# Output stores begun by ScalarE one unit late, and GpSimd's power two slots later, in a fused attention and MLP kernel

## The chip, the cores and the metric

The kernel runs on one NeuronCore of a Trainium2 chip. A core has five engines that each take their instructions in order: TensorE (PE, matmuls), VectorE (DVE), ScalarE (ACT), GpSimd (POOL) and SyncE (SP, which here only begins transfers). They wait for one another through semaphores. The metric is the device time of one execution in microseconds, as the median of several; less is better.

## What is computed

For 8 batches of 8 heads, 576 positions and head width 64: causal attention with a bias from a running sum, then a layer norm over the 512 joined columns, a two-layer MLP (512 to 2048 to 512, ReLU) and a residual.

```python
scores = q @ k.T / sqrt(64)
cum = cumsum(maximum(s, 0));  bias = minimum(-(cum_i - cum_j), 0)
attn = softmax(where(causal, -1e9, scores + bias))
x = (attn @ v)                      # heads joined: (8, 576, 512)
mu, var = mean(x), mean((x - mu) ** 2)
xn = (x - mu) / sqrt(var + 1e-6) * g_ln
out = x + maximum(xn @ w_ch1, 0) @ w_ch2
```

The power in the title is the `(var + 1e-6) ** -0.5` of the layer norm, the deviation. The kernel applies it last: it scales the MLP's result by `rstd` as it adds the residual, which is allowed because ReLU and the matmuls keep a positive factor per row.

## The kernel before

The main loop goes over 64 slots n = 8 b + h, one for each head h of batch b. A slot makes the scores of its head (`sa`, `sb`, `sc`, and in even slots `sd` for the last 64 positions of two heads), their exponentials on ScalarE, the causal masks on GpSimd, and the product with v (`pot`) of the head two slots back. Between these it works off a queue of MLP units of the batch before: 16 units `mlp1` (four matmuls each) and, for each of four row tiles, four units `mlp2`. From batch 3 on a slot takes four units; the `mlp1` units fall into h = 4 to 7 and the `mlp2` units into h = 0 to 3 of the next batch. Two pools of PSUM matter here, each with two buffers, and one SBUF pool of three for finished rows:

```python
yop  = tc.tile_pool(name="yop", bufs=3)
ps_m = tc.tile_pool(name="ps_m", bufs=2, space=PSUM)     # ph and py of the MLP
ps_t = tc.tile_pool(name="ps_t", bufs=2, space=PSUM)     # sd and trx
```

The last block of scores, and the transposes of the normalised rows; both take a buffer of `ps_t`:

```python
def scores_d(b, j):
    ...
    d = ps_t.tile([P, 2, TL], F32, name="sd", tag="tr")
    ...                                            # matmuls into d
    nc.scalar.activation(out=ed, in_=d[0:TL], func=ACT.Exp, scale=scale)
    ...

def ln_tr(b, t, eng="dve"):
    ...
    tr = ps_t.tile([P, KD, P], BF16, name="trx", tag="tr")
    for kd in range(KD):
        nc.tensor.transpose(tr[:, kd, :], xn[:, kd * P : (kd + 1) * P], ident)
    ...
    copy_on(eng, dst, tr)
```

The layer norm's pieces. VectorE does the statistics and `xn`; after the last tile `ln_rstd` adds 1e-6 on VectorE and takes the power on GpSimd:

```python
    def ln_rstd(b):
        n = len(x_tiles(b))
        rs = rstd[:, b, 0:n]
        nc.vector.tensor_scalar_add(out=rs, in0=mvs[b][:, 0:n, 1], scalar1=1e-6)
        nc.gpsimd.tensor_tensor(out=rs, in0=rs, in1=mhalf[:, 0:n], op=ALU.pow)

    def ln_xn(b, t):
        ...                                        # ln_aggr, xn on VectorE
        if b > 0 and t == len(tiles) - 1:
            ln_rstd(b)
```

The last quarter of a tile's `mlp2` finishes its rows on VectorE and hands them to `put`, which begins the store on SyncE:

```python
        if quarter == 3:
            yo = yop.tile([P, Dm], F32, name="yo", tag="yo")[:, 0 : c1 - c0]
            nc.vector.scalar_tensor_tensor(
                out=yo, in0=py[0], scalar=rs, in1=x[:, c0:c1], op0=ALU.mult, op1=ALU.add
            )
            dst(yo, c0, c1)
...
    def batch_units(b):
        def of_t(t):
            def put(yo, c0, c1):
                nc.sync.dma_start(out=out[b, t * P : (t + 1) * P, c0:c1], in_=yo)
            return xb[b][:, t, :], rstd[:, b, t : t + 1], put
        return chunk_units(lambda: xTs[b], of_t)

...
    def run_units(n, dve_first=False):
        for i in range(n):
            if queue:
                first_unit[0] = dve_first and i == 0
                queue.pop(0)()
```

The rows of 64 that are left over from each batch are gathered in pairs and done at the end (`mixed_units`); their stores are begun by SyncE and ScalarE already.

The body of a slot from n = 9 on, and the order within it (the loads and DMA transposes of coming heads, all on SyncE, are begun in `pre(n)`):

```python
def pv_next():
    ...
    pv(pb, ph_)
    ...
    if ph_ == 7:
        ln_open(pb)
        ...
        for t in range({1: 3, B - 1: 1}.get(pb, NT)):
            ln_xn(pb, t)

for n in range(BH):
    b, h = n // H, n % H
    pre(n)
    ...
        scores(b, h)
        run_units(1, True)
        if h % 2 == 0:
            scores_d(b, h // 2)
        run_units(1)
        if n > 9:
            pv_next()
        ...
        lt = {2: (0, 1), 3: (2, 3, 4)}.get(h, ()) if b > 1 else ()
        for t in lt:
            ln_tr(b - 1, t, "act" if b == 2 else "dve")
            if t != 1 and t != 4:
                run_units(1)
                nu -= 1
        ...
        run_units(nu)
        if b > 1 and h == 3:
            run_units(len(queue))
            queue += batch_units(b - 1)
```

So the layer norm of batch b - 1 runs on VectorE in h = 1 of batch b, two slots after its last head, and its transposes stand in h = 2 and h = 3.

Of the kernel before, what the change touches and what calls it, by code (L numbers as in the profile page):

```python
# [15 lines left out]
P = 128  # L16
# [3 lines left out]
def kernel(  # L20
# [11 lines left out]
    nc = tc.nc  # L32
    B, H, S, D = q.shape
# [43 lines left out]
    rstd = const.tile([P, B, NT], F32, name="rstd")  # L77
# [18 lines left out]
    def copy_on(eng, out, in_):  # L96
        if eng == "act":
            nc.scalar.copy(out=out, in_=in_)
        elif eng == "dve":
            nc.vector.tensor_copy(out=out, in_=in_)  # L100
        else:
            nc.gpsimd.tensor_copy(out=out, in_=in_)  # L102
# [140 lines left out]
    def tr_pair(g):  # L243
        tr_kind("k", g)
        tr_kind("q", g)
# [29 lines left out]
    def qk_pair(g, k_engs, q_engs):  # L275
        tr_pair(g)
        evac_pair("k", g, k_engs)
        evac_pair("q", g, q_engs)
# [62 lines left out]
    def scores_d(b, j):  # L341
        u0 = (2 * j) % 4
        pe_mask = b * H + 2 * j < NM
        ed = er[0:TL, u0 : u0 + 2, OD : OD + TL]
        d = ps_t.tile([P, 2, TL], F32, name="sd", tag="tr")
        for u in range(2):
            nc.tensor.matmul(
                d[:, u, :],
                lhsT=k_cols(b, 2 * j + u, NF),
                rhs=q_cols(b, 2 * j + u, NF * P, S)[0][2],  # L350
                start=True,
                stop=not pe_mask,
            )
            if pe_mask:
                nc.tensor.matmul(  # L355
                    d[:, u, :], lhsT=ident, rhs=maskT[:, 0:TL], start=False, stop=True
                )
        nc.scalar.activation(out=ed, in_=d[0:TL], func=ACT.Exp, scale=scale)
        if pe_mask:
            return  # L360
        nc.gpsimd.affine_select(
            out=ed,
            in_=ed,
            compare_op=ALU.is_ge,
            fill=0.0,
            base=0,
            pattern=[[0, 2], [1, TL]],
            channel_multiplier=-1,
        )
# [40 lines left out]
    def x_tiles(b):  # L410
        ts_ = [xb[b][:, t, :] for t in range(NF)]
        if b % 2 == 1:
            ts_.append(xm[b // 2])
        return ts_
# [20 lines left out]
    def ln_rstd(b):  # L435
        n = len(x_tiles(b))
        rs = rstd[:, b, 0:n]
        nc.vector.tensor_scalar_add(out=rs, in0=mvs[b][:, 0:n, 1], scalar1=1e-6)  # L438
        nc.gpsimd.tensor_tensor(out=rs, in0=rs, in1=mhalf[:, 0:n], op=ALU.pow)  # L439

    def ln_aggr(b, t):
        nc.vector.bn_aggr(out=mvs[b][:, t, :], in_=st[b][:, t, 0 : 4 if b == 0 else 3, :])
# [30 lines left out]
    def ln_first_rstd():  # L473
        for t in range(NF):
            ln_aggr(0, t)
        ln_rstd(0)

    def ln_tr(b, t, eng="dve"):
        if (b, t) not in xns:
            return  # L480
        xn = xns.pop((b, t))
# [3 lines that stand above are left out]
        if t < NF:  # L485
            dst = xTs[b][:, :, t * P : (t + 1) * P]
        else:
            dst = xTm[:, :, (b // 2) * P : (b // 2 + 1) * P]
        copy_on(eng, dst, tr)
# [40 lines left out]
    def chunk_units(xT_of, of_t, last=False):  # L530
        units = [lambda fb=fb: mlp1(xT_of(), fb) for fb in range(FB)]
        for t in range(NF):
            halves = ((0, 256), (256, 512)) if last and t == NF - 1 else ((0, 512),)
            for c in halves:
                for qr in range(4):
                    units.append(lambda t=t, qr=qr, c=c: mlp2(t, qr, *of_t(t), *c))
        return units

    def batch_units(b):
        def of_t(t):  # L540
            def put(yo, c0, c1):
                nc.sync.dma_start(out=out[b, t * P : (t + 1) * P, c0:c1], in_=yo)
            return xb[b][:, t, :], rstd[:, b, t : t + 1], put
        return chunk_units(lambda: xTs[b], of_t)

# [7 lines left out]

    queue = []
    pend = []

    def run_units(n, dve_first=False):
        for i in range(n):
            if queue:
                first_unit[0] = dve_first and i == 0  # L560
                queue.pop(0)()

# [30 lines left out]
    for i in range(2):  # L595
# [5 lines left out]
        out=maskT,  # L601
        in_=maskT,
# [18 lines left out]
    for t in range(NT):  # L621
# [5 lines left out]
        out=c_in, in0=c_in, scalar1=0.0, scalar2=1.0 / scale, op0=ALU.max, op1=ALU.mult  # L627
    )
    nc.vector.tensor_tensor_scan(
        out=c_sc, data0=c_one, data1=c_in, initial=0.0, op0=ALU.mult, op1=ALU.add  # L630
# [114 lines left out]
# [3 lines that stand above are left out]
        if n < 8:  # L748
            scores(b, h)
            if h in (1, 3, 5, 6):  # L750
                scores_d(b, h // 2)
            if h in (0, 2, 4):
                qk_pair(h // 2 + 1, ("dve", "dve"), ("act", "dve" if h < 4 else "act"))
            pend.append((b, h))
            if n == 7:
                pv_next()
                tr_pair(4)
                pv_next()
                evac_pair("k", 4, ("act", "act"))
                evac_pair("q", 4, ("act", "act"))  # L760
                trc = bias_tr()
                keep_warm(8)
                continue
            if n % 2 == 1 or n == 0:
                keep_warm(2)
            if n > 1:
                pv_next()
            if n == 6:
                pv_next()
            continue  # L770
        if n == 8:

            phs = [
                pool.tile([P, 512], F32, name="ph", tag=tag)
                for pool, tag in ((ps_m, "m"), (ps_m, "m"), (ps_s, "s"), (ps_s, "s"))
            ]

            def columns(t):
                cols = slice(t * P, (t + 1) * P)
                for fb, ph in enumerate(phs):  # L780
                    for kd in range(KD):
                        nc.tensor.matmul(
                            ph[:, cols],
                            lhsT=w1_bf[:, kd, fb * P : (fb + 1) * P],
                            rhs=xTs[0][:, kd, cols],
                            start=(kd == 0),
                            stop=(kd == KD - 1),
                        )

            for t in range(NF):  # L790
                ln_tr(0, t, "act" if t < 3 else "dve")
                if t > 0:
                    columns(t - 1)
            columns(NF - 1)
            for fb, ph in enumerate(phs):
                if fb % 2 == 0:
                    nc.scalar.activation(out=hT[:, fb, :], in_=ph, func=ACT.Relu)
                else:
                    nc.vector.tensor_scalar_max(out=hT[:, fb, :], in0=ph, scalar1=0.0)
            ln_first_rstd()  # L800
            queue += batch_units(0)[4:]
            scores(b, h)
            scores_d(b, h // 2)
            pend.append((b, h))
            run_units(1)
            continue

        end = next(m for m in (8 * i + 3 for i in range(2, B + 1)) if m >= n)
        nu = (2 if n < 16 else -(-len(queue) // (end - n + 1))) - 2
        if n in PAIRS:  # L810
            qk_pair(PAIRS[n], ("dve", "dve"), ("act", "act"))
# [7 lines that stand above are left out]
        if n == 9:  # L819
            bias_rows(trc)  # L820
        pend.append((b, h))
# [6 lines that stand above are left out]
        if n == 2 * H + 2:  # L828
            for t in range(3, NT):
                ln_xn(1, t)  # L830
        run_units(nu)
        if b > 1 and h == 3:
            run_units(len(queue))
            queue += batch_units(b - 1)
    pv_next()
# [3 lines left out]
    for t in range(NT):  # L839
        ln_xn(B - 1, t + 1)  # L840
        run_units(1)
        ln_tr(B - 1, t, "act")
    run_units(len(queue))
    queue += batch_units(B - 1)
    queue += mixed_units()
# [30 lines left out]
```

The softmax here doesn't subtract the row's maximum and nothing guards it: scores larger than these inputs give would overflow.

## Time and profile before

| what | value |
|---|---|
| time, median of 3 | 367.94 us (367.81 to 368.48) |
| span of the profiled run | 366.8 us |
| mean granted TensorE clock | 0.998 |
| TensorE busy (matmuls) | 97% of the span |
| VectorE, ScalarE, GpSimd busy | 55%, 52%, 45% |
| store of finished rows (`out_dram<-yo`) by SyncE | 32 of 256 KB, 0.36 us median to begin one |
| GpSimd's power (`rstd<-rstd,mhalf`) | 8, 1.1 us each |

In the profile's lines PE is TensorE, PEld its weight loads, DVE is VectorE, ACT ScalarE, POOL GpSimd and SPq SyncE's queue. L followed by a number is the line of the kernel. `py<-w_bf,hT` names what is written and what is read. Timeline lines begin with the start and the duration in microseconds; x8 at the end counts instructions merged into one line; a bracket gives the idle time before it and what ended it. In the list of waits the three numbers are microseconds in total, the number of waits and the longest.

### The profile page before, as it was taken

Reading aid. Unit: us, or ns where it says so; the run is one execution under the profiler, and the core shown is the slowest. Engines: PE = TensorE matmul, PEld = TensorE weight load, DVE = VectorE, ACT = ScalarE, POOL = GpSimd, SP = SyncE. Lnnn points to the kernel's source line nnn. Section 1 sums busy time; section 2 is a strip of 40 time slices with the busy share of each in tenths; the row PEclk is TensorE's granted clock in tenths of the full one; section 3 lists DMA queues with packets and bytes.
Section 4 is the critical chain, followed back from the end, with each engine's and each line's share of the span. In section 5 each row is a group of like instructions: output and inputs, shape, how many; then the busy total and the mean of one; then the engine's idle time right before and its main releaser. Section 6 shows DMA issues by size and latency. Waiting matters only on the chain.

```text
span 366.8 us, 8315 instructions
## 1 busy us (share of the span) xinstructions
PE 355.0 (97%) x3017; PEld 197.1 (54%) x3067; DVE 202.9 (55%) x535; ACT 191.3 (52%) x367; POOL 164.9 (45%) x447
## 2 busy tenths in 40 slices
PE   8998999999999999999999999999999999999995
PEld 3677555565555555555455555555555554444444
DVE  7697789684357554944384547743675483112211
ACT  5895988467732673367534753476337522501410
POOL 8854468667633656344675563554852101000000
PEclk9999999999999999999999999999999999999999
DMA  8999999999965999599979986798830011011013
GB/s 144 162 195 178 202 211 193 163 240 176 183 146 141 206 199 181 104 215 163 188 176 213 194 183 140 189 191 182 174 102 2 0 59 57 1 58 59 0 31 86
DMA packets 156653, 52.17 MB, mean 142 GB/s; under 512 B 143641, under 2 KB 151940, under 8 KB 156612
## 3 DMA queue, kind: packets, MB, share of 16 engines
q1 hardware_dynamic: 138868, 43.08, 55.5%
q0 software_dynamic: 17344, 8.03, 18.9%
q8 instruction: 24, 0.39, 0.5%
q10 hardware_dynamic: 400, 0.52, 0.4%
q14 instruction: 17, 0.14, 0.2%
HBM read 37.11 MB, written 9.44 MB: 127 GB/s over the span
## 4 chain that ended last, share of the span: by engine, by line
PE 72%; DVE 7%; DMA 6%; SPq 4%; POOL 4%; issue 3%; ACT 3%; POOLq 0%; ACTq 0%
PE py L515 26%; PE ph L497 25%; PE pot L389 6%; SPq L164 3%; PE sc L312 3%; PE sa L312 3%; PE sb L312 3%; DMA rowtmp<-in_q_dram 2%; PE idle L568 2%; DMA vtmp<-in_v_dram 2%; DVE xn L451 2%; PE trx L484 2%; DVE stats L423 1%; POOL er L331 1%; ACT er L323 1%
## 5 line engine op out<-in xcount | busy, mean ns | idle before, releaser
L515 PE MATMUL py<-w_bf,hT 128*128 128x512 bf16 (+1 forms) x565 | 132.1, 373 | 1.6 <-DVE yo L524 0.4
L497 PE MATMUL ph<-xT,w_bf 128*128 128x512 bf16 x478 | 116.4, 379 | 1.1 <-DVE yo L524 0.2
L507 ACT ACTIVATE hT<-ph 128x512 bf16<-128x512 f32 x102 | 61.0, 598 | 64.4 <-PE ph L497 64.4
L515 PEld LDWEIGHTS <-hT 128*128 128x128 bf16 x592 | 53.5, 98 | 49.1 <-issue 0.9
L497 PEld LDWEIGHTS <-w_bf 128*128 128x128 bf16 x560 | 50.1, 97 | 51.3 <-issue 2.9
L323 ACT ACTIVATE er<-sa 128x512 bf16<-128x512 f32 x64 | 38.2, 597 | 70.9 <-PE sa L312 50.1
L331 POOL TENSOR_SCALAR_AFFINE_SELECT er<-er 128x128 bf16<-128x128 bf16 x216 | 59.7, 300 | 22.5 <-ACT er L323 22.3
L505 DVE TENSOR_SCALAR hT<-ph 128x512 bf16<-128x512 f32 x38 | 26.3, 692 | 56.7 <-PE ph L497 49.0
L176 POOL CAST rows<-rowtmp 128x512 bf16<-128x512 f32 (+1 forms) x55 | 33.5, 609 | 50.7 <-DMA rowtmp<-in_q_dram 46.0
L312 PEld LDWEIGHTS <-kq 68*128 68x128 bf16 x452 | 33.4, 97 | 27.4 <-issue 1.7
L389 PEld LDWEIGHTS <-er 128*128 128x128 bf16 x960 | 37.5, 98 | 14.9 <-issue 0.7
L389 PE MATMUL pot<-v_bf,er 128*128 128x65 bf16 x960 | 40.2, 193 | 0.5 <-PE sd L355 0.3
L397 DVE RECIPROCAL rinv<-pot 128x5 f32<-128x5 f32 x64 | 12.3, 192 | 49.2 <-PE pot L389 48.9
L323 ACT ACTIVATE er<-sc 128x512 bf16<-128x512 f32 x64 | 39.2, 612 | 0.0
L323 ACT ACTIVATE er<-sb 128x512 bf16<-128x512 f32 x64 | 38.4, 599 | 0.3 <-PE sb L312 0.2
L524 DVE SCALAR_TENSOR_TENSOR yo<-py,rstd,xb 128x512 f32<-128x512 f32 x32 | 23.9, 748 | 26.2 <-PE py L515 19.7
L399 DVE TENSOR_TENSOR xb<-pot,rinv 128x256 f32<-128x256 f32 x64 | 27.2, 425 | 2.2
L102 POOL CAST v_bf<-vtmp 128x512 bf16<-128x512 f32 (+1 forms) x30 | 18.5, 617 | 19.6 <-DMA vtmp<-in_v_dram 19.5
L439 POOL TENSOR_TENSOR rstd<-rstd,mhalf 128x4 f32<-128x4 f32 (+1 forms) x8 | 8.8, 1095 | 38.0 <-DVE rstd L438 37.9
L312 PE MATMUL sc<-kq 68*128 68x256 bf16 (+1 forms) x216 | 25.3, 229 | 0.3
L423 DVE BATCH_NORM_STATS2 stats<-xb 128x6 f32<-128x128 f32 (+2 forms) x100 | 25.3, 313 | 0.4
L312 PE MATMUL sb<-kq 68*128 68x64 bf16 (+1 forms) x172 | 24.5, 244 | 0.9 <-DMA kq<-rows 0.6
(101 smaller groups left out, 322.1 us busy)
## 6 DMA issues: line engine op xcount, KB each, us to landing
out_dram<-yo SPq DMA_DIRECT2D x32, 256.0 KB
vtmp<-in_v_dram SPq DMA_DIRECT2D x24, 256.0 KB
rowtmp<-in_k_dram SPq DMA_DIRECT2D x44, 128.0 KB
rowtmp<-in_q_dram SPq DMA_DIRECT2D x44, 128.0 KB
w_bf<-in_moe_w_ch_dram POOLq DMA_DIRECT2D x8, 512.0 KB, 10.7
kp<-in_k_dram POOLq DMA_DIRECT2D x9, 144.0 KB, 6.8
qp<-in_q_dram POOLq DMA_DIRECT2D x9, 144.0 KB, 7.0
v_bf<-in_v_dram POOLq DMA_DIRECT2D x8, 128.0 KB, 8.1
```

The costliest lines, as they stand in the source:

```text
L176: nc.gpsimd.tensor_copy(out=r[0:pn, :, :, 0:D], in_=loaded.pop(("rows", gam, t))[0:pn])
L312: nc.tensor.matmul(a[:, c + a0 - q0 : c + a1 - q0], lhsT=k_cols(b, h, kb), rhs=cols, start=True, stop=not (pe_mask and diag),)
L323: nc.scalar.activation(out=e[:, o : o + 512], in_=a, func=ACT.Exp, scale=scale)
L331: nc.gpsimd.affine_select(out=e[:, o : o + P], in_=e[:, o : o + P], compare_op=ALU.is_ge, fill=0.0, base=0, pattern=[[1, P]], channel_mult ...
L389: nc.tensor.matmul(pot[:, t, :], lhsT=e[:, o : o + P], rhs=vv[:, kb, h, :], start=(kb == 0), stop=(kb == last),)
L399: nc.vector.tensor_tensor(out=xb[b][:, :, hs], in0=pot[:, 0:NF, 0:D], in1=rinv[:, 0:NF].unsqueeze(2).to_broadcast([P, NF, D]), op=ALU.mult,)
L423: nc.vector.bn_stats(out=st[b][:, t, part, :], in_=x[:, lo:hi])
L497: nc.tensor.matmul(ph, lhsT=w1_bf[:, kd, fb * P : (fb + 1) * P], rhs=xT[:, kd, :], start=(kd == 0), stop=(kd == KD - 1),)
L505: nc.vector.tensor_scalar_max(out=hT[:, fb, :], in0=ph, scalar1=0.0)
L507: nc.scalar.activation(out=hT[:, fb, :], in_=ph, func=ACT.Relu)
L515: nc.tensor.matmul(py[0], lhsT=hT[:, fb, t * P : (t + 1) * P], rhs=w2_bf[:, fb, c0:c1], start=(fb == 0), stop=(fb == FB - 1),)
L524: nc.vector.scalar_tensor_tensor(out=yo, in0=py[0], scalar=rs, in1=x[:, c0:c1], op0=ALU.mult, op1=ALU.add)
```

## The change

A store on SyncE waits until VectorE has finished the rows, and the loads and transposes behind it in SyncE's queue wait too. The change takes the 32 stores of the whole row tiles out of that queue. `put` now only notes the store; `run_units` begins the noted stores on ScalarE after the next unit, so that the rows have one unit's time to be finished. Secondly the power is cut off from `ln_rstd` and issued at the end of h = 3 instead of h = 1, so that GpSimd doesn't stand at it while VectorE is still at the layer norm. No arithmetic changes.

```diff
--- before.py
+++ after.py
@@ -436,6 +436,11 @@
         n = len(x_tiles(b))
         rs = rstd[:, b, 0:n]
         nc.vector.tensor_scalar_add(out=rs, in0=mvs[b][:, 0:n, 1], scalar1=1e-6)
+
+
+    def ln_pow(b):
+        n = len(x_tiles(b))
+        rs = rstd[:, b, 0:n]
         nc.gpsimd.tensor_tensor(out=rs, in0=rs, in1=mhalf[:, 0:n], op=ALU.pow)
 
     def ln_aggr(b, t):
@@ -474,6 +479,7 @@
         for t in range(NF):
             ln_aggr(0, t)
         ln_rstd(0)
+        ln_pow(0)
 
     def ln_tr(b, t, eng="dve"):
         if (b, t) not in xns:
@@ -539,7 +545,7 @@
     def batch_units(b):
         def of_t(t):
             def put(yo, c0, c1):
-                nc.sync.dma_start(out=out[b, t * P : (t + 1) * P, c0:c1], in_=yo)
+                stores.append((out[b, t * P : (t + 1) * P, c0:c1], yo))
             return xb[b][:, t, :], rstd[:, b, t : t + 1], put
         return chunk_units(lambda: xTs[b], of_t)
 
@@ -553,12 +559,18 @@
 
     queue = []
     pend = []
+    stores = []
+
 
     def run_units(n, dve_first=False):
         for i in range(n):
             if queue:
                 first_unit[0] = dve_first and i == 0
+                held = list(stores)
+                stores.clear()
                 queue.pop(0)()
+                for dst, src in held:
+                    nc.scalar.dma_start(out=dst, in_=src)
 
 
 
@@ -830,6 +842,7 @@
                 ln_xn(1, t)
         run_units(nu)
         if b > 1 and h == 3:
+            ln_pow(b - 1)
             run_units(len(queue))
             queue += batch_units(b - 1)
     pv_next()
@@ -840,6 +853,7 @@
         ln_xn(B - 1, t + 1)
         run_units(1)
         ln_tr(B - 1, t, "act")
+    ln_pow(B - 1)
     run_units(len(queue))
     queue += batch_units(B - 1)
     queue += mixed_units()
```

## The prediction

> **What bounds the kernel now.** I read the page's busy shares and 40 slices, then who waits for whom (engines, then SyncE's queue), then the timeline of each engine around single slots.
>
> ```profile
> PE 355.0 (97%) x3017; PEld 197.1 (54%) x3067; DVE 202.9 (55%) x535; ACT 191.3 (52%) x367; POOL 164.9 (45%) x447
> PE   8998999999999999999999999999999999999995
> ```
>
> TensorE is busy 355.0 of 366.8 us, at a granted clock of 0.998, and full in all but the first and last slices. Only 11.8 us are idle, most of it in the first 60 us and at the end. The kernel is bound by TensorE's in-order stream. A change to stores can win only where they hold TensorE up, and can lose anything it makes TensorE wait.
>
> I take a slot's length from the start of one slot's `sa` matmul to the next. From batch 3 on a slot without transposes takes 4.63 or 4.57 us, h = 2 takes 5.08, h = 3 takes 5.02 with two transposes and about 5.25 with three. Five slots are longer: batch 4 h = 3 (5.62), h = 4 (4.79), h = 7 (5.34), batch 5 h = 0 (5.42), batch 6 h = 3 (5.62). Their excess, 0.37 + 0.16 + 0.77 + 0.79 + 0.37 = 2.46 us, is what a better order could recover in the steady part.
>
> Next, the waits of SyncE's queue and one of GpSimd's (total us, times, longest):
>
> ```profile
> SPq L542 <- DVE yo L524: 41.7, 12, 17.5
> SPq L542 <- DVE mv L442: 26.0, 2, 24.7
> SPq L542 <- DVE rinv L397: 20.9, 7, 5.1
> ...
> POOL rstd L439 <- DVE rstd L438: 37.9, 7, 13.7
> ```
>
> L542 is the store. SyncE stands at it for up to 5 us per batch in the middle (the longest waits lie in the tail, where nothing is behind them), and loads and DMA transposes queue behind it. This is TensorE's timeline in batch 4, from h = 2 (sa at 145.92) into h = 3 (sa at 151.00):
>
> ```profile
> 147.45 0.22 PE L347 MATMUL sd<-kq 68*128 68x64 bf16 x2
> 147.51 1.03 PE L515 MATMUL py<-w_bf,hT 128*128 128x512 bf16 x4
> 148.37 0.62 PE L389 MATMUL pot<-v_bf,er 128*128 128x65 bf16 x15
> 148.83 0.39 PE L484 MATMUL trx<-ident,xn 128*128 128x128 bf16 x4
> 149.06 1.03 PE L515 MATMUL py<-w_bf,hT 128*128 128x512 bf16 x4
> 149.92 0.39 PE L484 MATMUL trx<-ident,xn 128*128 128x128 bf16 x4
> ...
> 152.04 1.89 PE L515 MATMUL py<-w_bf,hT 128*128 128x512 bf16 x8 [0.21 <-DVE yo L524]
> ```
>
> VectorE, ScalarE and SyncE in the same stretch:
>
> ```profile
> 151.04 0.16 DVE L438 TENSOR_SCALAR rstd<-mv 128x5 f32<-128x5 f32 x1
> 151.24 0.75 DVE L524 SCALAR_TENSOR_TENSOR yo<-py,rstd,xb 128x512 f32<-128x512 f32 x1
> ```
>
> ```profile
> 147.84 0.27 ACT L358 ACTIVATE er<-sd 64x128 bf16<-64x128 f32 x1
> 151.48 0.60 ACT L323 ACTIVATE er<-sa 128x512 bf16<-128x512 f32 x1 [3.37 <-PE sb L312]
> ```
>
> ```profile
> 146.33 0.57 SPq L139 DMA_DIRECT2D vtmp<-in_v_dram  x1
> 152.01 0.36 SPq L542 DMA_DIRECT2D out_dram<-yo  x1
> ```
>
> The reader should see: the rows of tile 1 are finished by TensorE at the end of h = 1 (about 146), but VectorE has the next batch's statistics and five normalised tiles ahead of them (145.4 to 151.2), so `yo` starts only at 151.24. SyncE waits for it 5 us. ScalarE does not care: it makes the exponential of `sd` at 147.84. What SyncE's lateness costs TensorE appears in h = 7 and the next h = 0:
>
> ```profile
> 173.28 1.11 PE L389 MATMUL pot<-v_bf,er 128*128 128x65 bf16 x15
> ...
> 176.94 0.40 PE L312 MATMUL sb<-kq 68*128 68x64 bf16 x3 [0.61 <-DMA kq<-rows]
> ```
>
> The first takes 1.11 us instead of 0.62: GpSimd's masks came late behind a late v load. The second waits for a transpose begun late.
>
> [...]
>
> **The change part by part.**
>
> 1. Taken from SyncE: 32 stores, 0.36 us median each, and their waits. By the built order of transfers, SyncE from batch 2 on then runs its loads as far ahead as the `kq` and staging buffers let it. I expect the late v load and transposes to vanish: 0.16 + 0.77 + 0.79 = 1.72 us won. The two 0.37 us are VectorE's lateness, not SyncE's.
>
> 2. GpSimd's power: 8 of 1.1 us, the same number. GpSimd waited 37.9 us in front of them, but its next work was mostly not yet ready (its masks wait for exponentials). In the new place `rstd` is ready. Worth about 0 by itself.
>
> 3. Put on ScalarE: 32 stores. Most stand in slots where it is idle for 3 us; 0.4 to 0.5 us each is hidden. One per batch is not. In the order of the changed kernel, ScalarE in h = 2 has sa, sb, sc, **the store of tile 1**, then the exponential of `sd`. One unit of delay is 0.87 us; `yo` of tile 1 is 5 us late. So the exponential of `sd` slips from 147.84 to after 151.99.
>
> That exponential frees a PSUM buffer. Pool `ps_t` has two: `sd` takes one, the first `trx` of the slot the other, the second `trx` needs that of `sd`; in the built program its first matmul waits for just this exponential. TensorE is in order, so it stands still. The second `trx` can start at: start of `yo` + 0.77 (to the store's start, as SyncE shows: 151.24 to 152.01) + 0.43 (issue; 0.36 is the median on SyncE, 0.50 on ScalarE in the tail) + 0.08 (gap, chosen) + 0.27 (exponential) + 0.05 (to TensorE) = `yo` + 1.60. With the times before:
>
> - batch 3: yo 111.99, ready 113.59, second trx 112.19: 1.40
> - batch 4: 151.24, 152.84, 149.92: 2.92
> - batch 5: 189.94, 191.54, 189.94: 1.60
> - batch 6: 228.99, 230.59, 227.67: 2.92
> - batch 7: 266.27, 267.87, 266.00: 1.87
>
> Sum 10.71 us. Even batches normalise five tiles of the odd batch before them, hence the longer ones. In batches 4 and 6 the old 0.37 us in h = 3 is swallowed (yo is long done): -0.74. Batch 2 has its copies on ScalarE and tile bounds elsewhere; its late exponentials have slack: 0. In the tail `yo` of tile 0 ends at 298.0, before the copy at 298.76: 0.[...]
>
> Total: 10.71 - 0.74 - 1.72 = +8.25 us, so 367.94 + 8.25 = 376.2 us.
>
> **The rivals.**
>
> A. The intended one: the store is ready when its turn comes, the lead of SyncE counts. Gain 1.7 to 2 us: 366 us. For it: SyncE's waits and the late transposes. Against it: yo's start after the second trx in four batches and level with it in one.
>
> B. The stall comes, but nothing is won back, because SyncE is still late[...], or a store waits for a late load instead of `yo`: 378 to 381 us. For it: SyncE trailed by 4 us and more in batches 4 and 5. Against it: per four slots SyncE issues ten row loads at 0.55, five transposes at 1.35 and one or two v loads at 0.6, about 13.8 of 18.5 us, so without the stores' waits it catches up.
>
> C. The stall is absorbed by later slack: it would need idle TensorE time after it, and there is none but the 0.37s. 373 to 375 us if VectorE's chain runs faster. I see little for it.
>
> **Range and chances.** The mechanism is read from order and buffers; I give 90% to a stall in at least four batches. Its size hangs on the issue time (0.1 us is 0.5 in the sum) and on whether the 1.72 returns. That gives 373.6 to 378.2. The 2% line is 375.3, just below the middle: slower 0.65, same 0.33, faster 0.02.
>
> **What would show it.** Right: in h = 2 of batches 3 to 7 the second trx waits for the exponential of `sd`, 1.4 to 2.9 us; the exponential follows the store on ScalarE; h = 7 of batch 4 and h = 0 of batch 5 return to 4.57 and 4.63; SyncE no longer waits for `yo` before the tail. Wrong: slots h = 2 of 5.1 us, or the wait of the store ended by a transfer, or GpSimd's power in front of a mask that TensorE waits for.

## The result and the profile after

The changed kernel takes 379.41 us (median of four runs, 377.89 to 379.59); the kernel before takes 367.88 beside it. The ratio is 1.0304, 95% interval 1.0273 to 1.0334: 11.5 us slower. The forecast was 376.2 with a range of 373.6 to 378.2, so the direction was right and the size was not. The profiled execution after spans 377.9 us (before 366.8), so 11.1 us can be followed instruction by instruction.

The page of the changed kernel, busy shares, slices of TensorE and of its granted clock:

```profile
PE 357.1 (94%) x3017; PEld 198.2 (52%) x3067; DVE 203.3 (54%) x535; ACT 191.5 (51%) x367; POOL 168.5 (45%) x447
PE   8898999999989999799989997999989999999995
PEclk9999999999999999899999999899999999999999
```

TensorE's slices now have dips, and two slices of the clock row fall to 8. The busy time of TensorE grew by 2.1 us with the same 3017 instructions. Idle time alone would not do that; slower instructions would.

Engine waits of the changed kernel (total us, times, longest):

```profile
ACT er L358 <- DVE rinv L397: 18.2, 5, 4.6
POOL rstd L444 <- DVE rstd L438: 18.0, 2, 13.7
PE trx L490 <- DVE xm L406: 5.5, 2, 2.8
PE trx L490 <- ACT er L358: 3.8, 3, 1.3
```

Line 358 is the exponential of `sd`: it stands five times, once in each batch from 3 to 7, for up to 4.6 us. `trx` on TensorE stands five times too, 9.3 us in all, longer in two of the five. Those two are ascribed to `xm` on VectorE, which is only the last thing the profile saw end; in the program the first matmul of that `trx` waits for the exponential of `sd`, as in the other three. GpSimd's wait at the power fell from 37.9 to 18.0 us; the two waits that are left stand at the start (38.6) and near the end (313.6).

SyncE's own waits after:

```profile
SPq L555 <- DVE yo L530: 59.6, 5, 51.7
SPq L186 <- PE sb L312: 30.8, 8, 6.1
```

L555 is the store of the last units only. In the middle SyncE no longer waits for rows; it waits for `kq` buffers (L186), that is, it has run as far ahead as it may.

The timeline after, batch 4, from h = 2 (`sa` at 147.36) into h = 3 (`sa` at 155.38):

```profile
150.27 0.39 PE L490 MATMUL trx<-ident,xn 128*128 128x128 bf16 x4
150.50 1.03 PE L521 MATMUL py<-w_bf,hT 128*128 128x512 bf16 x4
...
152.75 0.75 DVE L530 SCALAR_TENSOR_TENSOR yo<-py,rstd,xb 128x512 f32<-128x512 f32 x1
...
153.53 0.34 ACTq L573 DMA_DIRECT2D out_dram<-yo  x1
...
153.97 0.27 ACT L358 ACTIVATE er<-sd 64x128 bf16<-64x128 f32 x1 [4.56 <-DVE rinv L397]
...
154.30 0.38 PE L490 MATMUL trx<-ident,xn 128*128 128x128 bf16 x4 [2.77 <-DVE xm L406]
...
156.60 3.01 PE L521 MATMUL py<-w_bf,hT 128*128 128x512 bf16 x8
```

The chain of the forecast is all there: `yo`, store, exponential of `sd`, second `trx`. Then comes the thing that was not in it: the eight matmuls at 156.60 take 3.01 us, and 1.89 before. The same stretch by windows (us, busy time and count of PE, PEld, DVE, ACT and POOL, then the granted clock, DMA share, GB/s):

```profile
149.00:151.50 2.50, 2.50 (x30) 1.41 (x28) 2.42 (x5) 0.42 (x1) 1.03 (x3) 1.00 1.31 223
151.50:154.30 2.80, 0.03 (x2) 0.00 (x1) 2.70 (x9) 0.27 (x1) 0.00 (x0) 1.00 0.57 93
...
155.00:158.50 3.50, 3.50 (x16) 1.62 (x15) 0.89 (x2) 1.57 (x3) 3.00 (x10) 0.57 0.45 66
```

TensorE is idle from 151.5 to 154.3 with the clock still at 1.00, goes back to work, and then gets 0.57 of its clock over 3.5 us (0.50 from 155.5 to 158.5). The idle time is paid once while TensorE waits and again after it.

The two other places of the forecast, h = 7 of batch 4 and h = 0 of batch 5 (timeline of TensorE):

```profile
178.53 0.62 PE L389 MATMUL pot<-v_bf,er 128*128 128x65 bf16 x15
...
180.93 0.38 PE L312 MATMUL sb<-kq 68*128 68x64 bf16 x3
```

Both waits are gone. Slot by slot, as in the forecast:

| slots | before, us | after, us | difference in sum | forecast |
|---|---|---|---|---|
| h = 2, batches 3, 5, 7 | 5.09, 5.08, 5.08 | 6.50, 6.50, 6.50 | +4.25 | +4.87 |
| h = 2, batches 4, 6 | 5.08, 5.09 | 8.02, 8.02 | +5.87 | +5.84 |
| h = 3, batches 4, 6 | 5.62, 5.62 | 6.93, 6.93 | +2.62 | -0.74 |
| batch 4 h = 4 and 7, batch 5 h = 0 | 4.79, 5.34, 5.42 | 4.62, 4.57, 4.64 | -1.72 | -1.72 |
| sum | | | +11.02 | +8.25 |

This covers the 11.1 us between the two profiles. The miss lies in one row: h = 3 of batches 4 and 6.

### The profile page after: what moved, and what is told of

Same layout as the page of the kernel before. It is cut to its first block, busy times and chain, and to the rows that moved or that the text cites. A ratio compares the mean times of both kernels' runs of the same rounds, so it can differ in the third digit from the quotient of the medians.

```text
span 377.9 us, 8315 instructions
## 1 busy us (share of the span) xinstructions
PE 357.1 (94%) x3017; PEld 198.2 (52%) x3067; DVE 203.3 (54%) x535; ACT 191.5 (51%) x367; POOL 168.5 (45%) x447
## 4 chain that ended last, share of the span: by engine, by line
PE 79%; DVE 11%; issue 2%; POOL 2%; ACT 2%; DMA 2%; ACTq 0%; POOLq 0%
PE ph L503 31%; PE py L521 27%; PE pot L389 7%; DVE xn L456 4%; PE sc L312 3%; PE sb L312 3%; PE sa L312 3%; PE trx L490 2%; DVE stats L423 2%; DMA v_bf<-in_v_dram 2%; DVE xb L399 1%; DVE yo L530 1%; POOL v_bf L147 1%; DVE mv L447 1%; PE ph L794 1%
## 5 line engine op out<-in xcount | busy, mean ns | idle before, releaser
L521 PE MATMUL py<-w_bf,hT 128*128 128x512 bf16 (+1 forms) x565 | 134.6, 378 | 1.2
L331 POOL TENSOR_SCALAR_AFFINE_SELECT er<-er 128x128 bf16<-128x128 bf16 x216 | 64.5, 312 | 87.9 <-ACT er L323 87.7
L312 PE MATMUL sa<-kq 68*128 68x512 bf16 x64 | 24.6, 384 | 1.1 <-DMA kq<-c 0.9
L490 PE MATMUL trx<-ident,xn 128*128 128x128 bf16 x144 | 13.8, 219 | 10.0 <-DVE xm L406 5.5
## 6 DMA issues: line engine op xcount, KB each, us to landing
w_bf<-in_moe_w_ch_dram POOLq DMA_DIRECT2D x8, 512.0 KB, 11.1
```

What stands on the lines that cost most here:

```text
L312: nc.tensor.matmul(a[:, c + a0 - q0 : c + a1 - q0], lhsT=k_cols(b, h, kb), rhs=cols, start=True, stop=not (pe_mask and diag),)
L331: nc.gpsimd.affine_select(out=e[:, o : o + P], in_=e[:, o : o + P], compare_op=ALU.is_ge, fill=0.0, base=0, pattern=[[1, P]], channel_mult ...
L521: nc.tensor.matmul(py[0], lhsT=hT[:, fb, t * P : (t + 1) * P], rhs=w2_bf[:, fb, c0:c1], start=(fb == 0), stop=(fb == FB - 1),)
```

## The experiments

Times are medians beside runs of the kernel before on the same chip; slot lengths are from one profiled execution each.

### The two halves of the change

`pow_only` is the kernel before with the power moved, and nothing else. `store_only` is the changed kernel with the power put back.

```
pow_only:    ln_rstd() without the power; ln_pow(b - 1) in h == 3, stores on SyncE
store_only:  ln_rstd() with the power; stores held one unit, begun by ScalarE
```

> The kernel before with only the second part of the change: GpSimd's power two slots later, stores on SyncE as before. My theory: the power was never on TensorE's path; 367.9 us within 0.4, all slots as before. Rival (GpSimd standing 38 us before the power delays the masks and casts and so the loads): the long slots of batches 4 and 5 get shorter, 366.2 us.

Measured: 367.93 against 367.16, ratio 1.0026 (1.0001 to 1.0051). Alone, the late power is worth next to nothing, a little to the worse: h = 3 of batches 4 and 6 took 5.81 and 6.03 us.

> The kernel after with the power put back to its old place, so only the stores move to ScalarE. My theory: all of the loss is the stores'; 379.4 us within 0.5, h = 2 of batches 3 to 7 at 6.5 and 8.0 us, h = 3 of batches 4 and 6 at 6.9 us. Rival (the late power holds GpSimd's masks and so ScalarE): 376 us or less.

Measured: 380.24 against 367.16, ratio 1.0347 (1.0320 to 1.0374). The loss belongs to the stores, and they are no better without the late power; whether they are worse, the two intervals leave open. In this kernel the stall in batch 3 was 2.28 us, and h = 3 behind it took 6.67 us instead of 5.02: the clock again, behind a shorter idle time.

### Is it the exponential behind the store?

`sd_first` hands the store over only behind the exponential of `sd`; all else is as after.

```diff
-        run_units(1, True)
+        late = []
+        run_units(1, True, late)        # held stores are put into late
         if h % 2 == 0:
             scores_d(b, h // 2)
+        for dst, src in late:
+            nc.scalar.dma_start(out=dst, in_=src)
         run_units(1)
```

> The kernel after with one exchange: in even slots the store noted before is begun after the exponential of sd instead of before it. ScalarE still waits for yo at the store, equally long. My theory (only the PSUM buffer that the exponential of sd frees holds TensorE up, and the halved clock follows from that standstill): h = 2 back to 5.08, h = 3 to 5.02 and 5.62, full clock, the late transposes gone: 366.2 us within 0.6. Rival (ScalarE's waiting itself costs, through the exponentials of the next slot): h = 2 or h = 3 stays over by 1 us or more, above 371 us.

Measured: 371.51 against 367.16, ratio 1.0114 (1.0084 to 1.0144). All five slots h = 2 are back at 5.08 or 5.09 us. So the store in front of the exponential is the cause of the stall, all of it. But the time is 5 us over what I had expected: h = 3 of batch 4 took 9.02 us and of batch 6 7.45. A second loss had come out from under the first.

`act_lag` gives the stores four units of delay in place of one, still on ScalarE.

```diff
-                held = list(stores)
-                stores.clear()
+                held = list(stores)                 # entries [4, dst, src]
                 queue.pop(0)()
-                for dst, src in held:
-                    nc.scalar.dma_start(out=dst, in_=src)
+                for entry in held:
+                    entry[0] -= 1
+                    if entry[0] == 0:
+                        stores.remove(entry)
+                        nc.scalar.dma_start(out=entry[1], in_=entry[2])
```

> The kernel after with stores begun by ScalarE four units behind their rows instead of one. My theory: in h = 2 the store of tile 1 stands at the end of the slot, behind the exponential of sd; no stall, 366.2 us within 0.6. Rival (issuing on ScalarE costs by itself, 32 times 0.35 us in a path): above 370 us.

Measured: 372.10 against 367.16, ratio 1.0131 (1.0107 to 1.0154). The same picture: h = 2 at 5.08, h = 3 of batches 4 and 6 at 7.45 and 9.11. Both times are those of the rivals (above 371 and above 370 us), but their reason, that waiting or storing costs ScalarE something by itself, is ruled out below by `sp_lag` and `act_lag_oldpow`. I read the cause further below; first the clock.

### Is it the clock?

`fill12` is the changed kernel with twelve matmuls of zeros on TensorE in front of the second `trx` of batches 4 and 6. They add zeros to the sum that is being built, so nothing computed changes. They fill the idle time and can start nothing earlier. `fill4` has four of them.

```diff
         for t in lt:
+            if t == 1 and b in (4, 6):
+                for _ in range(12):
+                    nc.tensor.matmul(py[0], lhsT=zeros[:, 0:P], rhs=zeros, start=False, stop=False)
             ln_tr(b - 1, t, "act" if b == 2 else "dve")
```

> The kernel after with 12 matmuls of zeros (128x512, added into the running py, so the result is the same) ahead of the second trx in h = 2 of batches 4 and 6, 2.6 us at full clock, where TensorE stood idle 2.8 us. My theory (the idle time of 2.8 us lets the clock fall to half for 3.4 us, which costs 1.7 us in each h = 3): h = 2 stays at 8.0, the clock stays at 1.0, h = 3 falls from 6.93 to about 5.25: 376.0 us within 0.5. Rival (h = 3 is long because its rows, copies or masks come late, and the clock reading is a by-product): h = 3 stays at 6.9, 379.4 us.

> As before with 4 matmuls of zeros instead of 12: about 1.9 us of idle time remains. Odd batches stand idle 1.3 us and keep the clock. My theory[...]: clock 1.0, h = 3 at 5.25, 376.0 us. [...]clock halved as before, 379.4 us.

Measured: `fill12` 376.57 against 366.73, ratio 1.0268 (1.0247 to 1.0289); `fill4` 376.78, ratio 1.0292 (1.0233 to 1.0351). The timeline of TensorE in `fill12`, batch 4:

```profile
151.21 2.75 PE L838 MATMUL py<-zeros 128*128 128x512 bf16 x12
154.15 0.38 PE L490 MATMUL trx<-ident,xn 128*128 128x128 bf16 x4 [0.18 <-DVE xm L406]
...
155.89 1.89 PE L521 MATMUL py<-w_bf,hT 128*128 128x512 bf16 x8
```

and its windows over the same stretch:

```profile
150.00:155.00 5.00, 4.82 (x37) 2.43 (x34) 4.72 (x12) 0.27 (x1) 0.91 (x4) 1.00 0.85 172
155.00:158.50 3.50, 3.50 (x38) 2.12 (x37) 0.95 (x2) 1.57 (x3) 3.12 (x10) 1.00 0.49 80
```

The slot h = 2 is as long as after (8.02), since the `trx` waits for the same store. But the clock stays at 1.00, the eight matmuls take 1.89 us again, and h = 3 takes 5.25 us in both batches, which is what the forecast had put there. Work that does nothing makes the kernel faster: the profiled execution spans 374.4 us in place of 377.9, and the two slots h = 3 make 3.36 of these 3.5 us. The medians differ by 2.8 us, though only by 1.7 when each is taken over the kernel before beside it (9.8 and 11.5 us), with four executions of each; the slots and the clock carry the argument. The halved clock is shown as the cause of the missed part.

In `fill4` the idle time left is 1.91 us, twice. In batch 4 the clock was halved behind it (h = 3 of 6.92 us), in batch 6 it was not (5.25): each of the two outcomes named in the expectation came once. Equal idle times with unequal ends also occur in `act_lag`, where TensorE waits 2.03 us in both batches:

```profile
153.44 1.89 PE L521 MATMUL py<-w_bf,hT 128*128 128x512 bf16 x8 [2.03 <-DVE yo L530]
...
231.40 3.46 PE L521 MATMUL py<-w_bf,hT 128*128 128x512 bf16 x8 [2.03 <-DVE yo L530]
```

The first goes on at full clock, the second is halved, and that is the step from 7.45 to 9.11 us (and to 9.02 in `sd_first`, where the eight matmuls of batch 4 take 3.46 us behind the same 2.03 us). The windows over the two waits of `act_lag` and what follows them (columns as above):

```profile
150.00:153.40 3.40, 1.41 (x12) 0.77 (x11) 3.33 (x6) 0.00 (x0) 1.05 (x3) 1.00 0.59 105
153.40:155.60 2.20, 2.16 (x23) 1.21 (x23) 2.02 (x6) 1.57 (x3) 0.69 (x3) 1.00 1.04 247
155.60:157.00 1.40, 1.40 (x20) 0.93 (x17) 1.13 (x4) 0.00 (x0) 1.40 (x3) 1.00 0.66 155
...
228.00:231.30 3.30, 1.36 (x12) 0.73 (x10) 3.23 (x6) 0.00 (x0) 1.01 (x3) 1.00 0.84 177
231.30:234.70 3.40, 3.30 (x9) 1.21 (x9) 2.07 (x7) 1.57 (x3) 1.83 (x5) 0.54 0.90 214
234.70:238.00 3.30, 3.30 (x39) 2.24 (x38) 1.93 (x6) 0.00 (x0) 2.43 (x6) 0.96 0.80 205
```

During both waits the clock reads 1.00; behind the first it stays there, behind the second it reads 0.54. In the changed kernel it is at half from 155.46 to 158.87 and from 237.38 to 240.79, 3.41 us each, behind idle times of 2.77 us. In `store_only` the half clock begins at 116.17, 157.13 and 239.05, behind idle times of 2.28, 2.70 and 2.70 us. What separates two waits of the same 2.03 us, or of the same 1.91 in `fill4`, is left open.

### The second loss: who makes `yo` late in h = 3?

`sp_lag` and `sp_lag1` leave ScalarE out: SyncE begins the stores, four units or one unit behind, with the late power.

```
sp_lag:   as act_lag, with nc.sync in place of nc.scalar
sp_lag1:  the same, with 1 in place of 4
```

> Stores begun by SyncE as in the kernel before, but four units behind their rows, the power late as in the kernel after. My theory: SyncE's loads of the slot stand ahead of the store then, the store of tile 1 waits little, the late transposes are gone, no ScalarE stall: 366.2 us within 0.6. Rival (what helps is that the stores leave SyncE's queue at all): 367.9 us, with the long slots of batches 4 and 5.

> The kernel after with the stores begun by SyncE instead of ScalarE, one unit behind as there. My theory: no stall of TensorE (SyncE makes no exponentials); the loads of the slot stand ahead of the store, so most of the old lateness is gone too: 366.2 to 367 us. Rival (one unit behind is itself what delays, through yo's buffers): above 370 us.

Measured: 370.56 against 366.73, ratio 1.0103 (1.0066 to 1.0139), and 371.04, ratio 1.0115 (1.0089 to 1.0140). Both expectations of about 366 missed, and ScalarE has no part in it. h = 3 of batch 4 took 7.57 us in both, so one unit of delay or four makes no difference there. VectorE, GpSimd and TensorE in `sp_lag`, batch 4:

```profile
148.25 0.76 DVE L456 SCALAR_TENSOR_TENSOR xn<-xb,mv,gb 128x512 bf16<-128x512 f32 x1
...
149.12 0.60 POOL L176 CAST rows<-rowtmp 128x512 bf16<-128x512 f32 x1
149.20 2.50 DVE L456 SCALAR_TENSOR_TENSOR xn<-xb,mv,gb 128x512 bf16<-128x512 f32 x1
149.68 0.20 POOL L177 COPY rows<-cT 128x32 bf16<-128x32 bf16 x1
...
149.83 0.61 POOL L176 CAST rows<-rowtmp 128x512 bf16<-128x512 f32 x1
150.39 0.20 POOL L177 COPY rows<-cT 128x32 bf16<-128x32 bf16 x1
150.54 0.61 POOL L102 CAST v_bf<-vtmp 128x512 bf16<-128x512 f32 x1
...
152.88 0.75 DVE L530 SCALAR_TENSOR_TENSOR yo<-py,rstd,xb 128x512 f32<-128x512 f32 x1
```

One `xn` takes 2.50 us in place of 0.75. It begins 0.08 us behind a cast of GpSimd and ends half a microsecond behind the last of a row of casts and copies. Everything behind it on VectorE is 1.75 us later, `yo` of tile 1 too, and TensorE waits 2.17 us for the accumulator that `yo` frees. An `xn` of 2.50 us stands in batch 4 of `sd_first`, `act_lag` and `sp_lag1` too, each time some 0.07 us behind the first of these casts, and once more in batch 6 of the first two.

In the kernel before, those casts stand behind the power in GpSimd's order, and GpSimd waits at the power until the layer norm is over. The late power takes that wait away. `sp_lag_oldpow` and `act_lag_oldpow` are the two kernels with four units of delay and the power at its old place.

```diff
 def ln_rstd(b):
     nc.vector.tensor_scalar_add(out=rs, in0=mvs[b][:, 0:n, 1], scalar1=1e-6)
+    nc.gpsimd.tensor_tensor(out=rs, in0=rs, in1=mhalf[:, 0:n], op=ALU.pow)
 ...
-            ln_pow(b - 1)          # in h == 3
```

> The kernel after with the stores begun by SyncE four units behind, and the power issued at its old place, in h=1. Theory (with the power two slots later GpSimd no longer waits at it through the layer norm, so the casts that stand behind the power in the kernel before now run beside xn on VectorE, and xn of 2.50 us instead of 0.75 delays yo of tile 1 and with it TensorE): GpSimd waits at the power again until rstd, no xn over 1.2 us, h=3 of batches 4 and 6 back to 5.3-5.8 us (7.57 and 6.46 with the late power), and 365.5 to 368 us. Rival (early loads alone bring the casts into the layer norm, wherever the power stands): xn of about 2.5 us in h=1 of batch 4, h=3 of 7.5 us, and 369.5 to 371.5 us.

> The same with ScalarE beginning the stores, four units behind. Theory: as with SyncE, no xn over 1.2 us, h=3 of batches 4 and 6 at 5.3-5.8 us, clock at 1.00 there, 366 to 368.5 us (372.1 with the late power). Rival (a store on ScalarE costs TensorE something of its own): over 370 us.

Measured: 366.76 against 367.23, ratio 0.9990 (0.9974 to 1.0006), and 367.27, ratio 1.0002 (0.9992 to 1.0012). Every `xn` in h = 1 of batches 3 to 7 takes 0.75 us, and h = 3 is at 5.62 in batches 4 and 6, as before. GpSimd stands at the power again, in `sp_lag_oldpow`:

```profile
153.16 1.17 POOL L439 TENSOR_TENSOR rstd<-rstd,mhalf 128x5 f32<-128x5 f32 x1 [7.29 <-DVE rstd L438]
153.91 1.89 PE L515 MATMUL py<-w_bf,hT 128*128 128x512 bf16 x8 [0.21 <-DVE yo L524]
```

With the right delay, stores on ScalarE cost nothing that shows: 367.27 is level with the kernel before.

Is it the wait, or the place of the power? `sp_lag_gate` keeps the late power and puts a copy of 128x5 elements at the power's old place, on GpSimd. Its output is used by nothing.

```diff
     nc.vector.tensor_scalar_add(out=rs, in0=mvs[b][:, 0:n, 1], scalar1=1e-6)
+    nc.gpsimd.tensor_copy(out=gate[:, 0:n], in_=rs)
```

> SyncE four units behind and the late power, as in the run of 370.6 us, and one small GpSimd copy of the deviation (128x5, its output used by nothing) at the place where the power stood before, so that GpSimd waits there again until the layer norm has ended. Theory (what protects the layer norm is that GpSimd waits, not where the power is): xn at 0.75 us, h=3 of batches 4 and 6 at 5.5-5.9 us, 366.3 to 367.8 us. Rival (the late power delays yo or the casts by itself): h=3 of 6.5-7.6 us and 369.5 to 371.5 us.

Measured: 366.87 against 367.32, ratio 0.9993 (0.9976 to 1.0010). In its timeline:

```profile
151.74 0.19 POOL L441 COPY gate<-rstd 128x5 f32<-128x5 f32 x1 [7.27 <-DVE rstd L440]
151.88 0.61 POOL L102 CAST v_bf<-vtmp 128x512 bf16<-128x512 f32 x1
...
152.52 1.89 PE L524 MATMUL py<-w_bf,hT 128*128 128x512 bf16 x8 [0.22 <-DVE yo L533]
```

A useless instruction of 0.19 us takes the time from 370.6 to 366.9, because it waits. The wait is what protects the layer norm; where the power stands is of no consequence here.

Then the casts by themselves. `casts3` is the kernel before with three casts on GpSimd ahead of the power of batches 3 and 5, whose output is used by nothing.

```diff
+        if b in (3, 5):
+            for _ in range(3):
+                nc.gpsimd.tensor_copy(out=spare, in_=gb)
         nc.gpsimd.tensor_tensor(out=rs, in0=rs, in1=mhalf[:, 0:n], op=ALU.pow)
```

> The kernel before, with nothing of the change, and three casts of 128x512 f32 to bf16 added on GpSimd ahead of the power of batches 3 and 5, so that they run beside the layer norm on VectorE (their output is used by nothing). Theory: one xn of 2.0 to 2.6 us (0.75 without), yo of tile 1 about 1.8 us later, h=3 of batches 4 and 6 at 7.2 to 7.6 us (5.62), +3.3 to +4 us in all: 370.4 to 371.5; with half the clock after the idle time up to 374. Rival (casts cost VectorE nothing, the late power costs by itself): 366.5 to 368 us and xn at 0.75 us.

Measured: 367.82 against 367.23, ratio 1.0024 (1.0007 to 1.0042). The expectation of 370.4 and more missed. Batch 6 of `casts3`:

```profile
223.82 2.64 POOL L443 CAST spare<-gb 128x512 bf16<-128x512 f32 x3
223.82 1.15 DVE L456 SCALAR_TENSOR_TENSOR xn<-xb,mv,gb 128x512 bf16<-128x512 f32 x1
225.15 0.83 DVE L456 SCALAR_TENSOR_TENSOR xn<-xb,mv,gb 128x512 bf16<-128x512 f32 x1
226.16 0.83 DVE L456 SCALAR_TENSOR_TENSOR xn<-xb,mv,gb 128x512 bf16<-128x512 f32 x1
```

Here both engines take longer: the three casts 2.64 us, where three of 0.61 would be 1.83, and the `xn` beside them 0.40, 0.08 and 0.08 us more than 0.75. So the loss is there, but most of it fell on GpSimd; h = 3 of batch 6 took 6.18 us, against 5.62 before. Why an `xn` took 2.50 us beside a row of casts and small copies in four kernels, and at most 1.15 beside three casts in a row, I have not settled. Neither the moment of the start nor the small copy between explains it alone: in batch 6 of `sp_lag` an `xn` begins 0.07 us behind a cast with a copy behind it, as in batch 4, and takes 1.08 us, and the copy 0.66.

### What is left of the wait in h = 3

Two attempts to have `yo` of tile 1 earlier, both with SyncE four units behind and the power at its old place. `yo_first` runs the MLP units of h = 1 ahead of the previous head's product with V. `xn_split` leaves the units where they are and moves `xn` of tiles 3 and 4 behind them.

```diff
 yo_first
+        if b > 1 and h == 1:
+            run_units(nu)
+            nu = 0
         if n > 9:
             pv_next()
 xn_split
-            for t in range({1: 3, B - 1: 1}.get(pb, NT)):
+            for t in range({1: 3, B - 1: 1}.get(pb, 3)):
                 ln_xn(pb, t)
 ...
         run_units(nu)
+        if b > 2 and h == 1:
+            for t in range(3, NT):
+                ln_xn(b - 1, t)
```

> SyncE four units behind and the power in its old place, and in h=1 of every batch from 2 on the MLP units of the slot run ahead of the previous head's product with V, so that yo of tile 1 stands ahead of the layer norm on VectorE. Theory (what is left of the wait in h=3 of batches 4 and 6, 0.3-0.6 us, is for a PSUM buffer that yo of tile 1 frees behind the layer norm): those slots fall from 5.6 to 5.2 us, other slots unchanged: about 1 us below the same without it, 365 to 367. Rival: the layer norm ends later by as much as the units take, the transposes of h=2 wait for xn, and the time is over 368 us.

> SyncE four units behind, the power at its old place, and the layer norm of h=1 split: xn of tiles 0 to 2 where they were, then the slot's MLP units with yo, then xn of tiles 3 and 4. Theory (TensorE waits in h=3 of batches 4 and 6 for yo, which stands behind all five xn): h=3 falls from 5.62 to 5.1-5.3 us, 365.6 to 366.5 us. Rival (yo waits for its matmuls, and holds up the two xn behind it): h=3 at 5.6 us or more, 366.5 to 368.5 us.

Measured: `yo_first` 368.30 against 367.23, ratio 1.0032 (1.0019 to 1.0044); `xn_split` 366.25 against 367.32, ratio 0.9989 (0.9967 to 1.0010). In `yo_first` h = 2 of batches 4 and 6 grew from 5.08 to 5.63 us and h = 3 fell only from 5.62 to 5.45. In `xn_split` h = 3 fell to 5.25 in both batches, and nothing else moved; VectorE and TensorE in batch 4:

```profile
148.10 0.75 DVE L451 SCALAR_TENSOR_TENSOR xn<-xb,mv,gb 128x512 bf16<-128x512 f32 x1
...
148.88 0.75 DVE L524 SCALAR_TENSOR_TENSOR yo<-py,rstd,xb 128x512 f32<-128x512 f32 x1
...
151.26 1.89 PE L515 MATMUL py<-w_bf,hT 128*128 128x512 bf16 x8
```

`yo` starts between the third and the fourth `xn`, and the eight matmuls wait for nothing. By the medians it is the fastest of all, 1.1 us under the kernel before; the interval of the ratio reaches 1, so a gain is not shown.

## Why the prediction missed

**The mechanism was right.** The store of tile 1 in front of the exponential of `sd` holds the second `trx` in h = 2 of batches 3 to 7, and of no others. Moving the store behind the exponential brings all five slots back (`sd_first`).

**Its size was nearly right.** 10.12 us measured, 10.71 forecast. The store's issue took 0.34 us on ScalarE, not 0.43. Batches 5 and 7 were set at 1.60 and 1.87 and came to 1.42, like batch 3; in batch 7 of the profile before, one `xn` of 1.20 us beside a cast had made `yo` late, as in the second loss.

**The 1.72 us won back came, in the profile.** The three slots are at 4.62, 4.57 and 4.64. But how long they were before hung on the execution. In two other kernels that leave the stores of the kernel before on SyncE, `pow_only` and `casts3`, their excess was 0.43 and 0.26 us, and `sp_lag_oldpow`, which has all of the lead and no stall, is 0.47 us under the kernel before by the medians. A gain read from waits for late transfers in a single profile is worth 0 to 1.7 us; the forecast took it whole into its sum and left its failing to come to the range.

**The step that failed** is "the old 0.37 us in h = 3 is swallowed: -0.74". An idle time of 2.92 us was taken to cost itself, and nothing behind it. The profile before has a case that goes further, at its very end, where TensorE's last matmul ends at 362.99:

```profile
361.83:365.24 3.41, 1.16 (x11) 0.79 (x9) 0.48 (x1) 0.00 (x0) 0.00 (x0) 1.00 0.45 126
365.24:366.80 1.56, 0.00 (x0) 0.00 (x0) 0.00 (x0) 0.00 (x0) 0.00 (x0) 0.50 0.02 4
```

From 365.24, 2.25 us later, the clock is at half, and the mean of 0.998 that the forecast quotes comes from it. In the changed kernel it was at half for 3.41 us behind idle times of 2.77 us, which costs half of that, 6.93 - 5.25 = 1.68 us, in each of two batches: 3.36 us. With -0.59 from the smaller stalls it makes the 2.8 us between the forecast's sum and the table's. `fill12`, in which the clock is kept up, takes 376.57 us, within 0.4 of the forecast. Part of that is luck: the kernel before beside it takes 366.73 and not 367.94, so `fill12` loses 9.8 us where the forecast had 8.25. An estimate from the 0.43 and 0.26 us above puts 1.3 to 1.5 of these 1.6 us down to the three slots that were long in the one profile.

**The late power, "worth about 0 by itself",** is so by itself (1.0026). It was also not a cause of the 11.5 us: without it the stores cost no less (1.0347 against 1.0304). But "its next work was mostly not yet ready" was true only while SyncE was late. Once the loads come early, GpSimd's wait is what keeps its casts out of the layer norm, and the late power costs 3.8 us (370.56 against 366.76) with SyncE, 4.8 (372.10 against 367.27) with ScalarE. By the slots it is 2.80 us in the profiled execution of `sp_lag`, which kept the full clock; in `act_lag` one slot of the two had the halved clock besides. In the changed kernel this stays hidden: the stall holds up the exponential that GpSimd's mask waits for, and the casts behind it come only at 154.56, past the layer norm.

**The rivals.** A, 366 us, did not come; both of its conditions, a store ready at its turn and the lead of SyncE, are met in the kernels with four units of delay, and with the power at its old place these are level with the kernel before. B named 378 to 381, which holds the result, but for a reason that was not the case: SyncE was no longer late. (Its count of SyncE's work, "about 13.8" us, is 12.9 to 13.5 by its own terms; nothing hangs on it.) C is out: the slots behind the two long stalls grew.

## What to carry to other kernels

The store begun on ScalarE waited for `yo` with the exponential behind it, for up to 4.6 us, and TensorE stood up to 2.77 us for the buffer: before a DMA is moved to a computing engine, look for what stands behind it there, and for the buffer which that frees. When a stall of TensorE is forecast at about 2 us or more, reckon with the half clock behind it: here it lasted 3.41 us and cost 1.7 us, behind all five waits of 2.28 to 2.77 us and behind three of the eight of 1.91 to 2.17 us. A wait on an engine that is not the bound can be a guard; before it is taken away, ask what the engine will do in that time and beside which instructions: here an `xn` took 2.50 us in place of 0.75 beside GpSimd's casts and copies.

## What was not expected of the hardware

- TensorE's clock was halved for 3.41 us behind each of the four idle times of 2.70 and 2.77 us in `store_only` and the changed kernel; it began between 0.3 us before work set in again and 1.4 us after. One of 2.28 us had it too, those of 1.91 and 2.03 us three times out of six, two of 2.17 us not, and those of 1.05 to 1.51 us never. What separates the equal ones is left open.
- An `xn` on VectorE took 2.50 us in place of 0.75 beside five short instructions of GpSimd, and a small GpSimd copy beside `xn` took 0.67 in place of 0.20 us (`sd_first`, batch 3). Which of the two took longer differed from case to case.

The second is seen in `sd_first`, VectorE and GpSimd:

```profile
111.33 1.33 DVE L456 SCALAR_TENSOR_TENSOR xn<-xb,mv,gb 128x512 bf16<-128x512 f32 x1
111.51 0.60 POOL L176 CAST rows<-rowtmp 128x512 bf16<-128x512 f32 x1
112.06 0.67 POOL L177 COPY rows<-cT 128x32 bf16<-128x32 bf16 x1
```
